# A fused attention and two feed-forward layers on one core: softmax left unscaled, splits and block sums exchanged between two engines

## The chip, the core and the metric

One core of a Trainium2 chip runs the whole program in one launch. The metric is device time in microseconds (us), the median of several runs. TensorE (PE) does matrix products, VectorE (DVE), ScalarE (ACT) and GpSimd (POOL) do elementwise work, and SyncE (SP) issues nearly all DMAs. Each engine runs its own instructions in program order and waits for others by semaphores.

## The reference, cut to what matters

```python
# attention over channels: N = 6016 tokens, C = 256
qn = q / (norm(q, axis=tokens) + 1e-6);  kn = k / (norm(k, axis=tokens) + 1e-6)
s = kn.T @ qn / tau                       # 256 x 256
a = exp(s - s.max(-1));  a /= a.sum(-1) + 1e-9
x = v @ a                                 # tokens x 256
# first feed-forward layer, 2048 wide
h = x @ w_in;  x = maximum(0.01 * h, h) @ w_out
# second feed-forward layer, 1536 wide
out = (1 / (1 + exp(-(x @ w_gate))) * (x @ w_val)) @ w_out2
```

q, k and v are float32; the five weight matrices arrive as float64 and are turned into float32 inside the program.

## The kernel before, in words

**Start.** q and k come in groups of 128-token rows (`GROUPS`, in units of 128 tokens). For each group ACT squares both, DVE adds the squares to two accumulators (GpSimd takes the last ones of k), and TensorE adds to two 128x256 halves of k.T q. `ORDER` says which group's products follow which group's arrival; the second half lags behind, and `REST` holds its last products, which run after the norm products (L334). Then come the norms, the scaled scores (`scaled`, L355), exp with its row sum in `zs`, and `turned` (L371): 1/sum on DVE, the row scaled by it, two transposes on TensorE, a copy to `eT`.

**W'.** x is never formed. Since x @ w_in = v @ (a @ w_in), the kernel makes W' = a @ w_in block by block: for block j of 256 columns, `w_prime` (L212) does four float32 products into a PSUM bank `wp`, one half of the rows per half of `eT`.

**Weights.** A `Unit` is one 256x256 float64 block (512 KB). `act` (L168) takes two ACT instructions, x and c, and `join` (L175) three on DVE: L178, L179 and L183. W_in blocks are joined into `win`, blocks of w_out are joined and split.

**Splits.** Every operand of the large products is a pair: high = a rounded copy (ACT), low = the value minus high (a subtraction on DVE or GpSimd). A product of two pairs is three matmuls: low x high, high x low, high x high.

**Pairs and groups.** Tokens go in 6 pairs of two 512-token halves (the last of 2 x 448). For each layer and pair, a group j takes 256 hidden columns: 8 groups per pair in layer one, 6 in layer two. `Core` does a 256x256 by 256x1024 block product with 7 block products and block sums; the first pair of layer one uses `Plain` (L478) with 8 block products and no sums, because its W' is only then being made. A group's hidden blocks are named 22, 12, 11, 21. Each gets its activation (ACT, `g`), then `parts` (L514): high `gh` on ACT, low `gl` on the engine named. TensorE multiplies them with w_out one group later (`sum`, L531): `sums(("22", "12"))` stands after the first half of the next group's core and `sums(("11", "21"))` after that.

**What sets the order.** The order is written out by hand (`manual_schedule`); there is no planner. In a group of the first pair (from L672) TensorE does core.begin (banks d, b), the previous group's 22 and 12, `w_prime(j + 2)` into bank b, the previous 11 and 21, core.end (banks a, c). DVE's row is: join two units, four block sums of W' (L242 to L245, used by later pairs), the low parts of W' (L236), the low part of those sums (L251). GpSimd makes all four `gl` (L518).

**Late weights.** During pairs two to five the 18 units of layer two are joined on DVE (`late_join`, L581); the 12 gate and value units also get four block sums (`sums_of`, L185, on DVE at L190), then high and low parts, and go to DRAM. Each stands in DVE's row ahead of the group's `c12` (L470), which empties bank c for the next group.

**End.** After the last group its four hidden blocks are split, multiplied in the order 22, 12, 11, 21 and stored.

Of the kernel before, what the change touches and what calls it, by code (L numbers as in the profile page):

```python
# [22 lines left out]
P = 128  # L23
# [15 lines left out]
GROUPS = [1, 1, 2] + [4] * 10 + [2, 1]  # L39

ORDER = [
# [3 lines left out]
]  # L45
REST = [[(1, 10), (1, 13)], [(1, 11), (1, 12), (1, 14)]]

WIDTH = [4] * 10 + [2, 2, 2, 1, 1]
# [10 lines left out]
def attention_two_ffn(ctx, tc, q, k, vT, tau, w_in, w_out1, w_gate, w_val, w_out2, outT):  # L59
# [93 lines left out]
    class Unit:  # L153
# [21 lines left out]
        def join(self, out=None):  # L175

            s = cv.tile([P, CH], I32, tag="s", name="s", bufs=3)
# [4 lines left out]
            out = s if out is None else out  # L182
            nc.vector.tensor_tensor(out, s, self.c, ALU.add)  # L183
# [28 lines left out]
    def w_prime(j, wp, halves=range(KC)):  # L212

        w = f32(win[j]).rearrange("p (a b) -> p a b", a=2)
        for i in halves:
            for jj in range(KC):
                nc.tensor.matmul(  # L217
                    wp[:, i * 256:(i + 1) * 256], eT[i][:, jj * P:(jj + 1) * P], w[:, jj, :],
                    start=jj == 0, stop=jj == KC - 1,
                )  # L220
        return wp
# [15 lines left out]

    def block_sums(src, out):

        a, o = blocks(src), blocks(out)  # L240
        tt = nc.vector.tensor_tensor
# [15 lines left out]
    with tc.manual_schedule():  # L257


        with ExitStack() as actx:  # L260
# [61 lines left out]
            ins[0].load(ew)  # L322
            tok.load()
            ins[1].load(ew)
# [4 lines left out]
            win[0] = ins[0].join()  # L329
# [15 lines left out]
            nc.vector.tensor_scalar_mul(rn[:, 0:2], rn[:, 0:2], rt)  # L345
            products(REST[0])

# [33 lines left out]

            scaled(0)
            ins[1].act()
            win[1] = ins[1].join()
            for w in (B12, B22):
                tok.high(w)
                tok.low(w, nc.gpsimd)
            products(REST[1])
            turned(0)
            for w in (B11, B21):  # L390
                tok.high(w)
                tok.low(w, nc.gpsimd)
            wp0 = [bank("y2", "wp"), bank("y3", "wp")]
            for j in range(2):
                w_prime(j, wp0[j], [0])
            scaled(1)
            outs1[0].act()
            turned(1)
            o1_0 = outs1[0].join()
            for j in range(2):  # L400
                w_prime(j, wp0[j], [1])
                new_weights(j, s_a)
                split_blocks(j, wp0[j])
            ins[2].act()
# [228 lines left out]
        for i, (kind, p, j) in enumerate(groups):  # L633
# [44 lines left out]
            if kind == 1 and p == 0:  # L678
                core = Plain(s1_t[j], a21_t[j], g.tok, n)
                core.begin()  # L680

                for w, jj, u in acted:
# [5 lines left out]
                acted = [soon.pop(0) for _ in range(min(2, len(soon)))]  # L688

                def act(which):  # L690
                    for _, _, u in acted[which:which + 1]:
                        u.act()
                        load_next()

                adds()
                sums(("22", "12"))
                wp = w_prime(j + 2, bank("b", "wp")) if j + 2 < G1 else None
                g22, g12 = g.act(core.c22, tmp_tile("g22")), g.act(core.c12, tmp_tile("g12"))
                g.parts("22", g22, nc.gpsimd)
                g.parts("12", g12, nc.gpsimd)  # L700
                act(0)
                if j == 0:
                    for jj in range(2):
                        wt = tmp_tile("wt")
                        nc.scalar.copy(wt, wp0[jj])
                        unsummed.append((jj, wt))
                now = [(jj, block_sums(wt, tmp_tile("ws"))) for jj, wt in unsummed[:2 if j else 1]]
                unsummed = unsummed[len(now):]
                highs()
                lows()  # L710
                if wp is not None:
                    wt = tmp_tile("wt")
                    nc.scalar.copy(wt, wp)
                    new_weights(j + 2, s_a if j + 2 < 3 else s_b)
                    split_blocks(j + 2, wt)
                    unsummed.append((j + 2, wt))
                for jj, o in now:
                    split_sums(jj, o)
                sums(("11", "21"))
                finish()  # L720
                core.end()
                g.leaky("11", core.c11, tmp_tile("g11"), nc.gpsimd)
                g.leaky("21", core.c21, tmp_tile("g21"), nc.gpsimd)
                act(1)
# [51 lines left out]
            else:  # L776
# [37 lines left out]
                g.parts("11", gated("11", val.a), nc.gpsimd)  # L814
# [33 lines left out]
```

## Time and profile before

| | |
|---|---|
| median of 3 runs | 1112.7 us (1111.83 to 1113.08) |
| the profiled execution | 1111.23 us |
| its span, first to last instruction | 1109.5 us |
| DVE busy | 792.9 us (71%) |
| ACT busy | 602.1 us (54%) |
| POOL busy | 524.7 us (47%) |
| granted TensorE clock | full in every slice |
| bytes moved | 84.00 MB, mean 76 GB/s |

The page divides the span into 40 slices. TensorE's row reads 9 tenths or more in all but the first, the fifth and the last, which have 8. The shares of busy time are means over stages that differ, so the rows below are read stage by stage: the start (0 to 68 us), the first pair (68 to 157 us), the pairs with late weights (157 to 600 us), the rest, and the end.

### The profile page before, as it was taken

The page shows a single profiled execution, that of the slowest core. Times are in us where ns is not written, and L with a number is a line of the kernel's source. Part 1 is how long each engine was busy: PE and PEld are TensorE (multiplying, and loading weights), DVE is VectorE, ACT ScalarE, POOL GpSimd, SP SyncE. Part 2 cuts the span into 40 slices and gives each one's busy share as a digit, 9 for nine tenths or more (in the row PEclk, how much of TensorE's full clock was granted, in tenths as well). Part 3 has the DMA queues.
Part 4 walks back from the last instruction along what each step waited for, and adds up shares of the span by engine and source line. Part 5 has one row for each costly group of instructions (what it writes and reads, how often), then busy time and mean ns, then how long its engine had stood idle before and what let it go on. Part 6 is the DMA issues. An engine that isn't in the chain of part 4 may idle for free.

```text
span 1109.5 us, 13984 instructions
## 1 busy us (share of the span) xinstructions
PE 1083.4 (98%) x4842; PEld 906.1 (82%) x4842; DVE 792.9 (71%) x1100; ACT 602.1 (54%) x1043; POOL 524.7 (47%) x392
## 2 busy tenths in 40 slices
PE   8999899999999999999999999999999999999998
PEld 7778787878877788879988888888887888888997
DVE  7889956776786776783456687677677777668765
ACT  6666656676666676675564444444444344444433
POOL 0346566556655655656534434433433433443333
PEclk9999999999999999999999999999999999999999
DMA  9713212214223223209431002002002001100100
GB/s 349 248 38 114 78 57 76 79 77 149 91 76 109 86 91 124 90 34 360 161 118 40 1 0 77 1 1 76 1 1 77 1 1 38 34 1 1 39 1 34
DMA packets 31207, 84.00 MB, mean 76 GB/s; under 512 B 2976, under 2 KB 5792, under 8 KB 31136
## 3 DMA queue, kind: packets, MB, share of 16 engines
q1 hardware_dynamic: 31104, 83.11, 21.2%
q8 instruction: 38, 0.62, 0.2%
q14 instruction: 33, 0.27, 0.1%
q0 software_dynamic: 32, 0.00, 0.0%
HBM read 56.62 MB, written 26.48 MB: 75 GB/s over the span
## 4 chain that ended last, share of the span: by engine, by line
PE 86%; DVE 8%; issue 3%; ACT 2%; DMA 1%; POOL 1%; SPq 0%; DVEq 0%; ACTq 0%; POOLq 0%
PE c L441 13%; PE d L441 13%; PE a L441 12%; PE y L545 12%; PE y L542 12%; PE y L543 12%; PE b L441 6%; PE s L293 3%; DVE s L179 1%; DVE s L178 1%; DVE tok L144 1%; PE wp L217 1%; PE a L492 1%; DVE w L183 1%; DMA qt<-in_q 1%
## 5 line engine op out<-in xcount | busy, mean ns | idle before, releaser
L542 PE MATMUL y<-gh,wo 128*128 128x512 f32 (+1 forms) x672 | 260.1, 387 | 1.3 <-ACT gh L517 1.3
L543 PE MATMUL y<-gh,wo 128*128 128x512 f32 (+1 forms) x672 | 258.8, 385 | 0.0
L518 POOL TENSOR_TENSOR gl<-v,gh 128x512 fp32r<-128x512 f32 (+1 forms) x76 | 106.1, 1396 | 275.8 <-issue 187.2
L545 PE MATMUL y<-gl,wo 128*128 128x512 f32 (+1 forms) x672 | 205.0, 386 | 0.3 <-POOL gl L518 0.2
L441 PE MATMUL c<-tok,s 128*128 128x512 f32 (+1 forms) x672 | 186.7, 386 | 7.8 <-DVE c L470 7.8
L441 PE MATMUL d<-tok,s 128*128 128x512 f32 (+1 forms) x672 | 186.5, 386 | 0.0
L441 PE MATMUL a<-tok,s 128*128 128x512 f32 (+1 forms) x672 | 185.9, 385 | 0.0
L470 DVE TENSOR_TENSOR c<-u,c 128x512 f32<-128x512 f32 (+1 forms) x112 | 75.5, 675 | 134.6 <-PE c L441 129.4
L441 PEld LDWEIGHTS c<-tok,s 128*128 128x128 f32 x672 | 125.6, 188 | 33.5 <-DVE c L470 10.3
L518 POOL TENSOR_TENSOR gl<-g,gh 128x512 fp32r<-128x512 f32 (+1 forms) x72 | 98.0, 1370 | 104.5 <-PE d L441 70.4
L542 PEld LDWEIGHTS y<-gh,wo 128*128 128x128 f32 x672 | 126.2, 188 | 25.5 <-ACT gh L517 2.0
L545 PEld LDWEIGHTS y<-gl,wo 128*128 128x128 f32 x672 | 125.6, 188 | 25.9 <-POOL gl L518 2.8
L518 POOL TENSOR_TENSOR gl<-c,gh 128x512 fp32r<-128x512 f32 (+1 forms) x76 | 99.0, 1303 | 99.4 <-ACT gh L517 66.1
L441 PEld LDWEIGHTS d<-tok,s 128*128 128x128 f32 x672 | 125.6, 188 | 24.6 <-DVE u L475 1.6
L543 PEld LDWEIGHTS y<-gh,wo 128*128 128x128 f32 x672 | 126.2, 188 | 23.4
L441 PEld LDWEIGHTS a<-tok,s 128*128 128x128 f32 x672 | 126.2, 188 | 23.4
L455 DVE TENSOR_TENSOR u<-u,a 128x512 f32<-128x512 f32 (+1 forms) x112 | 75.1, 671 | 39.4 <-PE a L441 31.2
L518 POOL TENSOR_TENSOR gl<-u,gh 128x512 fp32r<-128x512 f32 (+1 forms) x76 | 98.6, 1297 | 0.0
L441 PE MATMUL b<-tok,s 128*128 128x512 f32 (+1 forms) x336 | 92.9, 385 | 0.0
L452 ACT COPY u<-b 128x512 f32<-128x512 f32 (+1 forms) x112 | 64.8, 578 | 47.5 <-PE b L441 47.5
L517 ACT CAST gh<-v 128x512 fp32r<-128x512 f32 (+1 forms) x76 | 46.5, 612 | 79.4 <-DVE v L803 76.2
L458 DVE TENSOR_TENSOR v<-u,c 128x512 f32<-128x512 f32 (+1 forms) x112 | 75.7, 676 | 14.2 <-PE d L441 0.5
(126 smaller groups left out, 1516.8 us busy)
## 6 DMA issues: line engine op xcount, KB each, us to landing
wr<-in_moe_w_out SPq DMA_DIRECT2D x14, 512.0 KB, 4.0
g_d<-st SPq DMA_DIRECT2D x6, 896.0 KB, 3.6
v_d<-st SPq DMA_DIRECT2D x6, 896.0 KB, 3.6
s<-g_d SPq DMA_DIRECT2D x6, 896.0 KB, 5.6
s<-v_d SPq DMA_DIRECT2D x6, 896.0 KB, 6.1
kt<-in_k SPq DMA_DIRECT2D x10, 512.0 KB, 9.7
qt<-in_q SPq DMA_DIRECT2D x10, 512.0 KB, 10.2
x_d<-o SPq DMA_DIRECT2D x20, 256.0 KB, 3.2
```

What stands on the lines that cost most here:

```text
L144: eng.tensor_tensor(t[:, 1], self.part(which), f32(t[:, 0]), ALU.subtract)
L293: nc.tensor.matmul(s_ps[i][:, :C], kt[:, t, i * P:(i + 1) * P], qt[:, t, :], start=i not in begun, stop=gi == ng - 1 and t == GROUPS[gi] - 1,)
L441: nc.tensor.matmul(o[:, :n], self.st[:, w, kind, :], t[:, x, :n], start=first and i == 0, stop=i == 2, skip_group_check=not first,)
L452: nc.scalar.copy(u[:, :n], self.b[:, :n])
L455: nc.vector.tensor_tensor(u[:, :n], u[:, :n], self.a[:, :n], ALU.add)
L458: nc.vector.tensor_tensor(v[:, :n], u[:, :n], self.c[:, :n], ALU.add)
L470: nc.vector.tensor_tensor(t[:, :n], self.u[:, :n], self.c[:, :n], ALU.add)
L517: nc.scalar.copy(gh[:, :n], src[:, :n])
L518: eng.tensor_tensor(gl[:, :n], src[:, :n], f32(gh[:, :n]), ALU.subtract)
L542: nc.tensor.matmul(acc[c, m][:, :n], wo[:, 1, e, s[m]], gh, start=first, stop=False)
L543: nc.tensor.matmul(acc[c, m][:, :n], wo[:, 0, e, s[m]], gh, start=False, stop=False)
L545: nc.tensor.matmul(acc[c, m][:, :n], wo[:, 0, e, s[m]], gl, start=False, stop=stop)
```

## The change

Five edits go together.

1. `GROUPS` begins 1, 1, 2, 2, 2 instead of 1, 1, 2, 4; `ORDER` no longer lets the second half lag in the first seven groups. `REST` keeps 6 and 9 products.
2. `turned` transposes the unscaled exp. 1/sum is computed beside it (`inverse`) and applied when W' leaves PSUM: as `scale` on ACT and as the scalar of one multiply-and-subtract on DVE (`split_half`, `w_evac`). The two halves of the first two W' blocks get banks of their own. W_in block 1 is loaded ahead of the tokens and its `act` moves ahead of the norms; the first join is cut in two.
3. In the first pair `gl` is made by DVE, and the block sums of W' by GpSimd. Token low parts at the start move from GpSimd to DVE.
4. In the first pair both units of a group are acted on and joined in the middle of that group, no longer at the beginning of the next. In group 0 core.end comes ahead of `w_prime(2)`.
5. The block sums of the late gate and value weights go to GpSimd. In the very last group the order is 22, 11, 12, 21, and the low part of 21 is made by DVE.

DVE at the start, from the reciprocal of the first row sum (`z_78`; `z_79` is the second) on. Before:

```order
L372 TENSOR_SCALAR z_78<-z_78 128x1
L373 RECIPROCAL z_78<-z_78 128x1
L374 TENSOR_SCALAR e<-e,z_78 128x256
L362 SCALAR_TENSOR_TENSOR s_sb<-s_123,rn,rq 128x256
L366 TENSOR_REDUCE nm<-s_sb 128x1
L372 TENSOR_SCALAR z_79<-z_79 128x1
L373 RECIPROCAL z_79<-z_79 128x1
L374 TENSOR_SCALAR e<-e,z_79 128x256
```

And now (`tok` are low parts of tokens, `wp` is W' in PSUM, `a_464` and `s` its split parts):

```order
L404 TENSOR_SCALAR z_78<-z_78 128x1
L405 RECIPROCAL z_78<-z_78 128x1
L386 SCALAR_TENSOR_TENSOR s_sb<-s_123,rn,rq 128x256
L390 TENSOR_REDUCE nm<-s_sb 128x1
L143 TENSOR_TENSOR tok<-raw,tok 128x512 x2
L176 TENSOR_SCALAR s<-wr 128x512
L177 SCALAR_TENSOR_TENSOR s<-x,s 128x512
L183 ISA s<-s,c 128x1024
L254 SCALAR_TENSOR_TENSOR a_464<-wp,z_78,a_464 128x128
L254 SCALAR_TENSOR_TENSOR s<-wp,z_78,s 128x128
L404 TENSOR_SCALAR z_79<-z_79 128x1
L405 RECIPROCAL z_79<-z_79 128x1
```

Both scalings of `e` are gone; token low parts and a join stand between the row maximum and the first low parts of W'.

DVE in a middle group of the first pair. Before (`wo` the rounded w_out block, `ws` the block sums of W', `wt` its copy in SBUF):

```order
L201 CAST wo<-s 128x512
L242 TENSOR_TENSOR ws<-wt 128x128
L243 TENSOR_TENSOR ws<-wt 128x128
L244 TENSOR_TENSOR ws<-ws,wt 128x128
L245 TENSOR_TENSOR ws<-wt,ws 128x128
L236 TENSOR_TENSOR a_839<-wt,a_839 128x128
L236 TENSOR_TENSOR s<-wt,s 128x384
L251 TENSOR_TENSOR s<-ws,s 128x512
L178 TENSOR_SCALAR s<-wr 128x512
L179 SCALAR_TENSOR_TENSOR s<-x,s 128x512
L183 ISA s<-s,c 128x1024
```

And now, with the row of the same W' block (`a_875`):

```order
L176 TENSOR_SCALAR s<-wr 128x512
L177 SCALAR_TENSOR_TENSOR s<-x,s 128x512
L183 ISA s<-s,c 128x1024
L206 CAST wo<-s 128x512
L242 TENSOR_TENSOR a_875<-wt,a_875 128x128
L242 TENSOR_TENSOR s<-wt,s 128x384
L549 TENSOR_TENSOR gl<-g_906,gh 128x512
L549 TENSOR_TENSOR gl<-g_912,gh 128x512
L273 TENSOR_TENSOR s<-ws,s 128x512
L549 TENSOR_TENSOR gl<-g_953,gh 128x512
```

Four `ws` rows have left DVE, four `gl` rows have come, and a unit's join stands ahead of the split of W' in the same group.

GpSimd where the first late gate unit (`w_1692`) is joined. Before:

```order
L126 TENSOR_TENSOR sums<-raw 128x1024
L518 TENSOR_TENSOR gl<-v,gh 128x512
L518 TENSOR_TENSOR gl<-g_1700,gh 128x512
L518 TENSOR_TENSOR gl<-c_1706,gh 128x512
L518 TENSOR_TENSOR gl<-u,gh 128x512
```

And now:

```order
L125 TENSOR_TENSOR sums<-raw 128x1024
L549 TENSOR_TENSOR gl<-v,gh 128x512
L195 TENSOR_TENSOR w_1692<-w_1692 128x128 x4
L549 TENSOR_TENSOR gl<-g_1722,gh 128x512
L549 TENSOR_TENSOR gl<-c_1728,gh 128x512
L549 TENSOR_TENSOR gl<-u,gh 128x512
```

The four sums stand between the low parts of 22 and 11, and wait for the join on DVE.

```diff
-GROUPS = [1, 1, 2] + [4] * 10 + [2, 1]
+GROUPS = [1, 1, 2, 2, 2] + [4] * 9 + [2, 1]
...
-WIDTH = [4] * 10 + [2, 2, 2, 1, 1]
+WIDTH = [4] * 11 + [2, 2, 2, 1, 1]
...
     def sums_of(w8):
...
-            nc.vector.tensor_tensor(w8[:, o], w8[:, a], w8[:, b], op)
+            nc.gpsimd.tensor_tensor(w8[:, o], w8[:, a], w8[:, b], op)
...
+    def split_half(j, i, wp):
+
+        src = wp.rearrange("p (a b) -> p a b", a=2)
+        st, a = s1_t[j], a21_t[j]
+        todo = [(st[:, :, 1:3], src)]
+        if i == 0:
+            todo = [(a[:, :, 0:1], src[:, 0:1]), (st[:, :, 0:1], src[:, 1:2])]
+        for o, x in todo:
+            nc.scalar.activation(o[:, 0], x, AF.Copy, scale=zs[i])
+        for o, x in todo:
+            nc.vector.scalar_tensor_tensor(o[:, 1], x, zs[i], f32(o[:, 0]), ALU.mult, ALU.subtract)
+
+    def w_evac(wt, wp):
+        for i in range(KC):
+            nc.scalar.activation(wt[:, i * 256:(i + 1) * 256], wp[i], AF.Copy, scale=zs[i])
+
     def block_sums(src, out):
...
-        tt = nc.vector.tensor_tensor
+        tt = nc.gpsimd.tensor_tensor
...
             ins[0].load(ew)
+            ins[1].load(ew)
             tok.load()
-            ins[1].load(ew)
...
             ins[0].act()
-            win[0] = ins[0].join()
+            ins[1].act()
+            ins[0].begin_join()
...
             def turned(i):
-                nc.vector.tensor_scalar_add(zs[i], zs[i], EPS_SUM)
-                nc.vector.reciprocal(zs[i], zs[i])
-                nc.vector.tensor_scalar_mul(e_sb[i], e_sb[i], zs[i])
...
             products(REST[1])
             turned(0)
...
+            wp0 = [[bank(f"y{2 + j}", "wp")[:, :256]] for j in range(2)]
+            for j in range(2):
+                w_half(j, 0, wp0[j][0])
+                new_weights(j, s_a)
+            scaled(1)
+            ins[2].act()
+            turned(1)
+            for w in (B12, B22):
+                tok.low(w, nc.vector)
+            o1_0 = outs1[0].join()
+            split_half(0, 0, wp0[0][0])
+            inverse(1)
+            for j in range(2):
+                wp0[j].append(w_half(j, 1, bank(f"y{j}", "wp")[:, :256]))
+            split_half(0, 1, wp0[0][1])
...
                 sums(("22", "12"))
+                if j == 0:
+                    core.end()
+                wp = w_prime(j + 2, bank("b", "wp")) if j + 2 < G1 else None
+                g22, g12 = g.act(core.c22, tmp_tile("g22")), g.act(core.c12, tmp_tile("g12"))
+                g.parts("22", g22, nc.vector)
+                g.parts("12", g12, nc.vector)
+
+                units = [soon.pop(0) for _ in range(min(2, len(soon)))]
+                for _, _, u in units:
+                    u.act()
+                    load_next()
...
+                if (p, j) == (NP_ - 1, count - 1):
+                    g.parts("12", gated("12", val.c12()), nc.gpsimd)
+                    g.parts("21", gated("21", val.c21()), nc.vector)
+                    g.sum(("22", "11", "12", "21"))
+                    g.store()
+                    break
```

## Rows read from the trace of the kernel before

**Rows 1.** The page, busy time of TensorE (us, share of the span, instructions).

```profile
PE 1083.4 (98%) x4842; PEld 906.1 (82%) x4842; DVE 792.9 (71%) x1100; ACT 602.1 (54%) x1043; POOL 524.7 (47%) x392
```

**Rows 2.** Waits of TensorE, whole run: us in total, times, longest.

```profile
PE c L441 <- DVE c L470: 7.8, 6, 1.8
PE wp L217 <- DVE s L183: 4.7, 3, 2.4
PE s L293 <- DMA qt<-in_q: 3.2, 2, 2.5
PE eT_ps L377 <- DVE e L374: 2.5, 2, 1.4
```

**Rows 3.** Timeline, 11 to 43 us: start, duration, engine, instruction [idle before, releaser].

```profile
11.87 30.89 PE L293 MATMUL s<-qt,kt 128*128 128x256 f32 x142 [2.54 <-DMA qt<-in_q]
...
42.28 0.42 DVE L314 TENSOR_TENSOR accq<-accq,s 128x256 f32<-128x256 f32 x1 [0.50 <-ACT x L171]
...
42.96 0.25 PE L334 MATMUL nrm<-ones,accq 128*128 128x1 f32 x1
```

**Rows 4.** Timeline, 40 to 70 us: softmax, W' and the first group.

```profile
46.51 4.05 PE L293 MATMUL s<-qt,kt 128*128 128x256 f32 x18
...
47.69 0.51 ACT L368 ACTIVATE e<-s_sb,nm 128x256 f32<-128x256 f32 x1
...
50.70 0.97 DVE L374 TENSOR_SCALAR e<-e,z 128x256 f32<-128x256 f32 x1
...
51.73 0.44 PE L377 MATMUL eT_ps<-ident,e 128*128 128x128 f32 x2 [1.17 <-DVE e L374]
...
52.63 1.99 PE L217 MATMUL wp<-s,eT 128*128 128x256 f32 x8 [0.46 <-ACT eT L380]
...
54.53 1.30 DVE L374 TENSOR_SCALAR e<-e,z 128x256 f32<-128x256 f32 x1
...
55.98 0.41 PE L377 MATMUL eT_ps<-ident,e 128*128 128x128 f32 x2 [1.35 <-DVE e L374]
...
58.66 0.97 PE L492 MATMUL d<-tok,a 128*128 128x512 f32 x3
...
63.11 1.97 PE L217 MATMUL wp<-s,eT 128*128 128x256 f32 x8 [1.02 <-DVE s L183]
```

**Rows 5.** Chain that ended last, 60 to 80 us: start, us, what.

```profile
67.82 1.36 PE d L492 x6
...
73.27 1.80 PE wp L217 x8
```

**Rows 6.** Groups by form, first pair (65 to 157 us): count, busy us, mean ns.

```profile
L243 DVE TENSOR_TENSOR ws<-wt 128x128 f32<-128x128 f32 x8 | 10.1, 1258 | 0.0
...
L251 DVE TENSOR_TENSOR s<-ws,s 128x512 fp32r<-128x512 f32 x8 | 5.4, 683 | 0.0
...
L242 DVE TENSOR_TENSOR ws<-wt 128x128 f32<-128x128 f32 x8 | 2.7, 338 | 2.1 <-ACT wt L705 2.1
```

**Rows 7.** The same, GpSimd.

```profile
L518 POOL TENSOR_TENSOR gl<-g,gh 128x512 fp32r<-128x512 f32 x30 | 44.2, 1494 | 14.9 <-ACT gh L517 8.5 <-issue 3.4 <-PE d L492 2.8
```

**Rows 8.** Windows: us, busy us (instructions) of PE, PEld, DVE, ACT, POOL, clock, DMA.

```profile
100.00:120.00 20.00, 18.77 (x83) 15.34 (x82) 19.42 (x22) 11.23 (x22) 13.95 (x10) 1.00 0.25 81
200.00:400.00 200.00, 194.38 (x852) 158.95 (x851) 149.62 (x196) 129.90 (x221) 115.52 (x82) 1.00 0.27 91
```

**Rows 9.** Timeline, 317 to 329 us, a late w_out unit.

```profile
326.69 0.96 PE L441 MATMUL c<-tok,s 128*128 128x512 f32 x3 [1.49 <-DVE c L470]
```

**Rows 10.** The same, 361 to 373 us, a gate or value unit.

```profile
368.29 1.99 DVE L190 TENSOR_TENSOR w<-w 128x128 f32<-128x128 f32 x4
...
370.93 0.97 PE L441 MATMUL c<-tok,s 128*128 128x512 f32 x3 [1.78 <-DVE c L470]
```

**Rows 11.** Groups by form, GpSimd, whole run: its smallest two-input form.

```profile
L314 POOL TENSOR_TENSOR acck<-acck,s 128x256 f32<-128x256 f32 x3 | 2.6, 877 | 0.2
```

**Rows 12.** Timeline, the end.

```profile
1101.27 0.47 PE L542 MATMUL y<-gh,wo 128*128 128x448 f32 x1 [1.30 <-ACT gh L517]
```

More of the change, by code (lines that the diff above doesn't have):

```diff
@@ L181, in join, with end_join @@
             )
-            out = s if out is None else out
-            nc.vector.tensor_tensor(out, s, self.c, ALU.add)
-            return out
+        def end_join(self, out=None):
+            out = self.s if out is None else out
+            nc.vector.tensor_tensor(out, self.s, self.c, ALU.add)
+            return out
+        def join(self, out=None):
+            self.begin_join()
+            return self.end_join(out)
     def sums_of(w8):
@@ L210, in attention_two_ffn, with w_half, w_prime @@
     win = {}
-    def w_prime(j, wp, halves=range(KC)):
+    def w_half(j, i, o):
         w = f32(win[j]).rearrange("p (a b) -> p a b", a=2)
[L215 to L221, printed above, removed]
+        for jj in range(KC):
+            nc.tensor.matmul(
+                o, eT[i][:, jj * P:(jj + 1) * P], w[:, jj, :], start=jj == 0, stop=jj == KC - 1
+            )
+        return o
+    def w_prime(j, wp):
+        return [w_half(j, i, wp[:, i * 256:(i + 1) * 256]) for i in range(KC)]
     ins = [Unit(cols(w_in, j)) for j in range(G1)]
@@ L380, in turned, with inverse @@
                 nc.scalar.copy(eT[i], eT_ps[:, :C])
+            def inverse(i):
+                nc.vector.tensor_scalar_add(zs[i], zs[i], EPS_SUM)
+                nc.vector.reciprocal(zs[i], zs[i])
             scaled(0)
-            ins[1].act()
             win[1] = ins[1].join()
+            inverse(0)
+            outs1[0].act()
             for w in (B12, B22):
                 tok.high(w)
-                tok.low(w, nc.gpsimd)
             products(REST[1])
             turned(0)
+            wp0 = [[bank(f"y{2 + j}", "wp")[:, :256]] for j in range(2)]
[13 more added lines that the diff above has]
+            split_half(0, 1, wp0[0][1])
             for w in (B11, B21):
                 tok.high(w)
[L392 to L404, printed above, removed]
+            split_half(1, 0, wp0[1][0])
+            split_half(1, 1, wp0[1][1])
+            for w in (B11, B21):
+                tok.low(w, nc.vector)
             win[2] = ins[2].join()
@@ L680, in attention_two_ffn @@
                 core.begin()
-                for w, jj, u in acted:
+                adds()
+                sums(("22", "12"))
+                if j == 0:
[8 more added lines that the diff above has]
+                    load_next()
+                if j == 0:
+                    for jj in range(2):
+                        wt = tmp_tile("wt")
+                        w_evac(wt, wp0[jj])
+                        unsummed.append((jj, wt))
+                now = [(jj, block_sums(wt, tmp_tile("ws"))) for jj, wt in unsummed[:2 if j else 1]]
+                unsummed = unsummed[len(now):]
+                for w, jj, u in units:
                     if w == "in":
@@ L687, in attention_two_ffn @@
                         split_rows(u.join(), o1_t[jj], nc.gpsimd)
[L688 to L708, printed above, removed]
                 highs()
@@ L716, in attention_two_ffn @@
                     unsummed.append((j + 2, wt))
+                sums(("11", "21"))
+                finish()
+                if j:
+                    core.end()
+                g.leaky("11", core.c11, tmp_tile("g11"), nc.vector)
+                g.leaky("21", core.c21, tmp_tile("g21"), nc.vector)
                 for jj, o in now:
                     split_sums(jj, o)
[L719 to L724, printed above, removed]
             elif kind == 1:
```

16 lines of the change are left out of this document (8 added, 8 removed), and 3 rows, old and new, of the table ORDER.

## The prediction

> **What bounds the kernel now.** I read the page first: TensorE is busy 98% of the span, 1083.4 of 1109.5 us [rows 1]. So nothing that merely frees another engine pays; at most the 26 us in which TensorE stands idle can be won. The list of TensorE's waits says where four of these lie: 7.8 us in six waits for DVE's c12 (L470), 4.7 in three for a join (L183), 3.2 for q, 2.5 for the scaled softmax [rows 2]. Then the timelines show which stage each falls in, and the windows whether the engine waited for is full there. In the first pair DVE is busy 19.42 of 20 us while TensorE is not [rows 8]: there DVE sets the pace. From 200 to 400 us DVE has 50 us to spare [rows 8], and the waits are places where too much stands ahead of one instruction.
>
> **First loads.** TensorE idles 2.54 us for q at 11.87 [rows 3], and smaller loads let its products start sooner. But the products end at 11.87 + 30.89 = 42.76, and DVE's last add of squares ends at 42.28 + 0.42 = 42.70; the norm product of q needs it and starts at 42.96 [rows 3]. TensorE runs in order, so products that finish sooner wait there. DVE's tail of adds is the same as before (the last three groups of four, then two and one). I cost this edit at 0; DVE's adds hide it. If the last add also comes sooner, at most the 2.54 are won; if the four extra small loads cost transfer rate, a little is lost. Range -0.3 to +2.5.
>
> **Softmax unscaled, start up to group 1.** Before, the last product ends at 46.51 + 4.05 = 50.56, and group 1's first matmul starts at 67.82 [rows 4, 5]: 17.26 us. The work of TensorE in between is 24 block matmuls, four times 1.36 per six = 5.44; three W' products at 1.80 (73.27 shows one without a stall) = 5.40; two pairs of transposes, 0.44 + 0.41 [rows 4, 5]. Together 11.69, so 5.57 is lost. Now the first exp, begun at 47.69, is ready before 50.56, and the scaling (0.97, begun at 50.70, and 1.30 at 54.53 [rows 4]) stands on no path to a transpose. So the waits of 1.17 and 1.35 in front of the transposes go, and DVE reaches the second half's scores 1 us sooner. What stays: both copies of the transposes to SBUF on ACT, 0.46 each [rows 4]. What is late next: the low parts. On DVE the low parts of two token blocks (0.68 each, as L251 [rows 6]) and a join of three instructions now stand ahead of the first low part of W', and `inverse(1)` behind it holds ACT's scaled copy of the second half; behind that copy ACT has two token highs, block 1's copies and the group's activations, for which TensorE waits next. I let TensorE lose 0.55 there. So 0.92 + 0.55 = 1.47 stays of 5.57: 4.1 won. core.end ahead of `w_prime(2)` covers the join that made TensorE wait 1.02 at 63.11 [rows 4]; that is part of the 5.57. Bounds: all but the copies, 4.65; or only the two waits on the scaling, 1.17 + 1.35 = 2.5, less 1 for the new queue on ACT and DVE, 1.5. Loading W_in block 1 ahead of the tokens puts three token transfers one block later on SP's queue; they are first read at the token highs, after block 1's x and c, so I give it nothing.
>
> **First pair.** Of the 4.7 waited for joins, 4.7 - 1.02 = 3.7 lie here [rows 2, 4]. Per group DVE loses four block sums (mean 0.338 to 1.258 each [rows 6]: 1.4 to 5.0) and gains four low parts at 0.683, as L251 of the same shape [rows 6], 2.7. GpSimd loses four at 1.494 [rows 7], 6.0, and gains four block sums. Their price on GpSimd isn't in the trace: the nearest form, two inputs of 256 columns, took 0.877 [rows 11]; below lies DVE's 0.338, above GpSimd's 1.494 for 512 columns. I take 0.6, 2.4 a group. The same block sum takes 0.338 or 1.258 on DVE as L242 or L243 [rows 6], which differ in what GpSimd does beside them. The Trainium skill (SBUF — State Buffer, Who interferes with whom) says that a DVE instruction with two SBUF inputs and a GpSimd one that reads SBUF exclude each other for the whole instruction; the two means agree. By that rule alone the sum over both engines counts, and it falls from 6.0 + 1.4 to 2.7 + 2.4, so relief would come all the same.
>
> The joins also stand half a group earlier than the product that needs them. So the 3.7 go. A new wait comes in group 1: ACT has six half-size scaled copies and four unit copies in group 0, its activations of group 1 stand behind them, and the W' product into bank b waits for the second. I let this cost 0.6, between nothing and one W' product, 1.8. The low parts on DVE are needed by TensorE half a group later and more. Net 3.1, between 1.5 and 3.7.
>
> **Late weights.** Two of the six waits, 2.9 together, are at w_out units, like the 1.49 at 326.69 [rows 9]; no block sum stands there and nothing changes. The other four, 7.8 - 2.9 = 4.9, are at gate and value units. At 368.29 four sums take 1.99 directly ahead of c12, and TensorE then waits 1.78 [rows 10]: without them c12 comes in time. On GpSimd they stand between the low parts of 22 and of 11, and make 11, 12 and 21 later by four sums and the wait for the join; 12 is wanted early in the next group. GpSimd idles 84 us in 200 [rows 8], so I allow 0.5 for this: 4.4 won, between 2 and 6.
>
> **End.** TensorE waits 1.30 for the high part of 12 [rows 12]. With 11 ahead of it, six matmuls fill that, and 12's gate no longer stands behind c21. 21's low part moves to DVE beside 12's on GpSimd. I take 1.1, between 0.4 and 1.8.
>
> **Sum.** 0 + 4.1 + 3.1 + 4.4 + 1.1 = 12.7. Against the profiled execution, 1111.23 (span 1109.5 and 1.7 around it), that makes 1098.5; this execution was 1.5 under the median, so from 1112.7 it makes 1100.0, which I predict. With the inner bounds it lies between 1097 and 1102.5.
>
> **Rivals.**
> *The work only changes places.* DVE and GpSimd exclude each other, and DVE, now with the low parts that TensorE waits for, stays full in the first pair: 3.1 becomes 0, and GpSimd's block sums cut the late gain in half, 2.2. 4.1 + 2.2 + 1.1 = 7.4: 1105.3. For it: DVE at 19.42 of 20 [rows 8] and the 1.258 [rows 6]. Against: a low part is less than half as long on DVE as on GpSimd (0.683 against 1.494). The Trainium skill (Perfetto Trace Analysis, Optimizing Scalar/DVE Operations) warns that moving operations between these two might not help, because they share a port; this is that case, and the exchange here goes the other way for the larger operations.
> *The start is eaten by its new queue.* The order on ACT and DVE behind the second exp is long; the start gives 1.5 and not 4.1: 1102.6. For it: each engine is in order and every new instruction ahead of a split counts. Against: the rows show DVE and ACT with gaps there only because of the scaling.
> *More goes than I count.* The last add of squares comes sooner (another 1.7), and the waits at w_out units go because their neighbours ran on time (2.9): 1095.4.
> *Slower: GpSimd becomes the bound.* If a sum of 128 columns costs GpSimd as much as 512 columns (a fixed cost), 1.494, the four take 6.0 in each of the 12 gate and value groups. A group of 45 matmuls takes 10.2 us, so GpSimd's idle time [rows 8] is 84.5 x 10.2 / 200 = 4.3 a group. 1.7 too much twelve times is 20, with nothing won in the first pair or the late ones: 1112.7 - 5.2 + 20 = 1127. It decides from 4.3 / 4 = 1.1 us a sum. Against it: 256 columns took 0.877 [rows 11].
>
> **Chances.** The forecast 0.60, work changes places 0.13, start eaten 0.14, more than counted 0.08, slower 0.05. The range, 1095.5 to 1106, takes in all but the slower rival and the far ends. No change (within 0.2%, 2.2 us, about what a measurement of this kernel can tell) would need several of the terms to fail together: 0.03. Faster 0.92, slower 0.05.
>
> **What would show it.** Right: no wait of a transpose for DVE; group 1's first matmul of bank d at 63.7 or so; no wait of a W' product for a join; c12 waits left at two w_out units alone; in the end TensorE's wait for gh under 0.4. The norm products still start close to 42.9, and TensorE waits there. A block sum on GpSimd lasts under 0.9. Wrong: norm products a microsecond earlier (first loads pay); W' products waiting for ACT's activation into bank b in several groups; `y` matmuls waiting for `gl` from DVE or GpSimd; DVE still at 95% in the first pair with TensorE waiting.

## The result and the profile after

The changed kernel takes 1094.26 us (median of 6 runs, 1093.51 to 1095.26) against 1112.99 for the kernel before (1111.83 to 1115.58): a ratio of 0.9829, 95% interval 0.9816 to 0.9841. The gain is 18.7 us where 12.7 were forecast; 1094.26 lies 1.2 us below the low end of the range.

The page after, busy time, answers to [rows 1]:

```profile
span 1091.4 us, 13956 instructions
...
PE 1081.2 (99%) x4842; PEld 907.2 (83%) x4842; DVE 774.6 (71%) x1059; ACT 604.6 (55%) x1055; POOL 522.2 (48%) x435
```

TensorE's waits after, whole run, answer to [rows 2] (us in total, times, longest):

```profile
PE c L472 <- DVE c L501: 2.9, 2, 1.5
PE idle L298 <- DVE ones L293: 1.1, 1, 1.1
PE wp L221 <- ACT eT L401: 0.9, 2, 0.5
PE s L315 <- DMA qt<-in_q: 0.9, 2, 0.7
PE nrm L357 <- DVE accq L336: 0.2, 1, 0.2
```

Gone are the 4.7 for joins and the 2.5 for the scaled rows; 7.8 for c12 became 2.9. The listed waits that went add up to 13.4 (4.9 + 4.7 + 2.5, and 1.3 at the end), about the forecast; q's 3.2 became 0.9 besides. The two spans differ by 18.1. So the waits were named rightly and something beside their listed length was won.

The start after, timeline (start, duration, engine, instruction), answers to [rows 3 to 5]:

```profile
40.34 0.50 PE L357 MATMUL nrm<-ones,acck 128*128 128x1 f32 x4
41.00 0.61 PE L357 MATMUL nrm<-ones,accq 128*128 128x1 f32 x4 [0.16 <-DVE accq L336]
...
44.57 4.05 PE L315 MATMUL s<-qt,kt 128*128 128x256 f32 x18
48.46 0.38 PE L398 MATMUL eT_ps<-ident,e 128*128 128x128 f32 x2
49.30 1.99 PE L221 MATMUL wp<-s,eT 128*128 128x256 f32 x8 [0.46 <-ACT eT L401]
51.13 0.38 PE L398 MATMUL eT_ps<-ident,e 128*128 128x128 f32 x2
...
61.35 1.04 PE L523 MATMUL d<-tok,a 128*128 128x512 f32 x3
```

The transposes follow the products at once, and group 1's first d comes soon after its W' product. Stage by stage, profile against profile and by the chain as in the prediction, the 18.1 us are:

| stage | forecast | between the two profiles |
|---|---|---|
| up to q's norm product (42.96, now 41.00) | 0 | 1.96 |
| last product to group 1's first d (17.26, now 13.08) | 4.1 | 4.18 |
| first pair from there (89.61, now 85.50) | 3.1 | 4.11 |
| pairs two on, to the third of the last three d products (940.96, now 934.50) | 4.4 | 6.46 |
| end (11.11, now 9.70) | 1.1 | 1.41 |

The windows after, in the columns of [rows 8]:

```profile
100.00:120.00 20.00, 20.00 (x90) 16.72 (x89) 19.31 (x25) 16.85 (x34) 12.42 (x12) 1.00 0.30 87
200.00:400.00 200.00, 198.40 (x873) 163.07 (x872) 144.10 (x172) 135.03 (x230) 131.85 (x113) 1.00 0.28 98
```

In the first pair DVE is as full as before, 19.31 of 20 us, and TensorE no longer waits for it. The GpSimd block sum of a late unit, whose price the prediction had to bound from [rows 11], and the low part of g on DVE in the first pair:

```profile
L195 POOL TENSOR_TENSOR w<-w 128x128 f32<-128x128 f32 x48 | 21.2, 463 | 17.3 <-DVE w L183 16.4
```

```profile
L549 DVE TENSOR_TENSOR gl<-g,gh 128x512 fp32r<-128x512 f32 x29 | 28.2, 1008 | 3.3 <-ACT gh L548 3.3
```

### The profile page after: what moved, and what is told of

It reads as the page before. It is cut to its first block, busy times and chain, and to the rows that moved or that the text cites. A ratio compares the mean times of both kernels' runs of the same rounds, so it can differ in the third digit from the quotient of the medians.

```text
span 1091.4 us, 13956 instructions
## 1 busy us (share of the span) xinstructions
PE 1081.2 (99%) x4842; PEld 907.2 (83%) x4842; DVE 774.6 (71%) x1059; ACT 604.6 (55%) x1055; POOL 522.2 (48%) x435
## 4 chain that ended last, share of the span: by engine, by line
PE 92%; DVE 4%; DMA 2%; ACT 1%; issue 1%; SPq 0%; ACTq 0%; DVEq 0%
PE c L472 13%; PE y L576 13%; PE d L472 13%; PE y L573 13%; PE y L574 13%; PE a L472 13%; PE b L472 7%; DMA kt<-in_k 2%; PE wp L221 1%; PE a L523 1%; PE c L523 1%; PE b L523 1%; PE d L523 1%; DVE accq L336 1%; PE s L315 1%
## 5 line engine op out<-in xcount | busy, mean ns | idle before, releaser
L491 DVE TENSOR_TENSOR v<-v,d 128x512 f32<-128x512 f32 (+1 forms) x112 | 75.7, 676 | 11.7
```

Source lines behind the costliest of these rows:

```text
L491: nc.vector.tensor_tensor(v[:, :n], v[:, :n], self.d[:, :n], ALU.add)
```

## The experiments

Times are medians; the changed kernel, timed again beside three of them, took 1093.47, and its ten timed runs have a median of 1093.9. The experiments ran on four chips. Runs of the kernel before whose clock stayed up have a median of 1110.0 on one of them and 1111.2 on another, so differences under about 1 us between runs that are not said to be beside each other say little, and I go by the traces there. "Excess" is worked out from the starts of neighbouring matmuls in the traces: what they stand further apart than the 0.227 of unhindered 512-column matmuls, summed around one wait. "Matmul for matmul" compares the starts of the same matmuls in two traces.

### First loads

The changed kernel with GROUPS, ORDER, REST and WIDTH of before, and the kernel before with those of the changed one:

```
-GROUPS = [1, 1, 2, 2, 2] + [4] * 9 + [2, 1]
+GROUPS = [1, 1, 2] + [4] * 10 + [2, 1]
```

> The changed kernel with the group sizes and the product order of the kernel before, all else as changed. Theory A (DVE's adds of squares run without a gap from the first groups of four on, one per 1.28 us as the loads do; whoever starts them 1.4 us sooner ends them that much sooner): the norm product of q goes back from 41.00 to about 42.9 and the run takes 1.9 to 2.0 us longer than the changed kernel, about 1096.2. Theory B (the prediction's step: the end of the adds doesn't depend on the first loads): no change, 1094.3, norm product of q still near 41.0.

> The kernel before with only the new group sizes and product order. Theory A: its norm product of q starts near 41.0 instead of 42.96 and it takes 1.9 us less than before, about 1111.0. Theory B (the adds hide it): same time as before, 1112.9.

Measured: 1093.96, no loss that a median shows, and 1111.14 beside 1111.79, ratio 0.9994 (0.9982 to 1.0005). The 1.9 of theory A falls. With the old loads the first square of four units came at 9.21, against 10.54 in the first profile of before, though the loads are the same:

```profile
9.21 1.06 ACT L333 ACTIVATE s<-kt 128x1024 f32<-128x1024 f32 x1 [1.05 <-DMA kt<-in_k]
```

```profile
10.54 1.06 ACT L310 ACTIVATE s<-kt 128x1024 f32<-128x1024 f32 x1 [3.03 <-DMA kt<-in_k]
```

The first row is of the changed kernel with old loads, the second of the kernel before. The norm product of q, with old loads in the changed kernel, then with new loads in the kernel before:

```profile
41.60 0.59 PE L358 MATMUL nrm<-ones,accq 128*128 128x1 f32 x4
```

```profile
40.75 0.61 PE L333 MATMUL nrm<-ones,accq 128*128 128x1 f32 x4 [0.17 <-DVE accq L313]
```

So much of the 1.96 was chance, but not all. The three profiles with old loads have this product at 41.60, 42.12 and 42.96, the fifteen with new loads between 40.58 and 41.58, 41.0 in the mean. By these means the edit is worth 1.2, by the two medians taken beside each other 0.6, and the interval of that ratio takes in nothing as well as 1.2. I take 0.6, somewhere from 0 to 1.2: theory B's "no change" isn't shown either.

### The kernel before once more

> The kernel before, unchanged, for a second profile and the granted clock of each of its runs. Theory A (two things of the first profile were chance: its first load of four units came late, at 10.54, and its clock didn't fall; most runs lose over 1 us more to a clock that falls to half behind one of TensorE's long waits): the first square of four units starts near 9.2, the norm product of q near 41.6, and runs with a mean clock of 0.998 or less take 1.5 to 3.5 us longer than those at 1.000. Theory B (the first profile is typical): 10.5, 42.9, and no relation between clock and time.

Measured: 1112.48 (1110.79 to 1114.09, 12 runs); the profiled one has a mean clock of 0.995. Its first square of four units starts at 9.24, as theory A has it, but its q norm product at 42.12, half a us later than A says: when the first load lands is not the whole of it. The clock's part of theory A holds. The profile shows what the first profile did not. TensorE behind the wait at 371.89 of the timeline, and the windows of 1 us around it (busy us of PE, PEld, DVE, ACT, POOL; granted clock; DMA):

```profile
371.89 0.96 PE L441 MATMUL c<-tok,s 128*128 128x512 f32 x3 [1.78 <-DVE c L470]
372.69 1.23 PE L441 MATMUL d<-tok,s 128*128 128x512 f32 x3
373.73 0.63 PE L542 MATMUL y<-gh,wo 128*128 128x512 f32 x1
...
376.66 0.39 PE L543 MATMUL y<-gh,wo 128*128 128x512 f32 x1
```

```profile
371.00:372.00 1.00, 0.11 (x1) 0.11 (x1) 0.90 (x3) 0.13 (x1) 0.00 (x0) 1.00 0.50 208
372.00:373.00 1.00, 1.00 (x4) 0.67 (x5) 1.00 (x2) 0.91 (x2) 0.00 (x0) 1.00 0.02 7
373.00:374.00 1.00, 1.00 (x4) 0.79 (x3) 0.87 (x2) 0.97 (x3) 0.71 (x1) 0.59 0.00 0
374.00:375.00 1.00, 1.00 (x3) 0.72 (x3) 0.73 (x2) 1.00 (x2) 1.00 (x2) 0.50 0.00 0
375.00:376.00 1.00, 1.00 (x4) 0.80 (x3) 0.73 (x1) 1.00 (x3) 0.82 (x1) 0.50 0.00 0
376.00:377.00 1.00, 1.00 (x5) 0.82 (x4) 1.00 (x2) 0.97 (x3) 0.00 (x0) 0.70 0.00 0
377.00:378.00 1.00, 1.00 (x6) 0.83 (x5) 0.37 (x1) 1.00 (x2) 0.98 (x1) 1.00 0.49 201
```

For 1.78 up to 371.89 TensorE waits; from 373.2 to 376.6 its granted clock stands at the lower level (0.50, 1.2 GHz), and a `y` matmul lasts 0.63 where one at the full clock lasts 0.39. The excess around this wait is 3.75; in the first profile, the clock at 1.00, it was 2.15. This execution has two more falls, at the waits that end at 50.89 (52.3 to 55.7) and at 127.64 (127.4 to 130.8). Of 66 runs of the kernel before in this study, 20 have a mean clock of 0.999 or 1.000, median 1110.7; 46 are lower, median 1113.2; the same order holds on each of the two chips that have many runs of both kinds (1110.0 against 1112.8, 1111.2 against 1113.3). Of ten runs of the changed kernel none is below 0.999.

### Late block sums back on DVE

```
-            nc.gpsimd.tensor_tensor(w8[:, o], w8[:, a], w8[:, b], op)
+            nc.vector.tensor_tensor(w8[:, o], w8[:, a], w8[:, b], op)
```

> The changed kernel with the four block sums of a late gate or value unit back on DVE. Theory A (each listed wait for c12 costs TensorE about 0.35 more than its listed length, and each of four such waits comes back): 6.0 to 6.5 us longer than the changed kernel, 1100.3 to 1100.8. Theory B (the listed lengths are the cost): 4.9 us longer, 1099.2. The listed waits of c for c12 should read about 7.8 in six by both.

Measured: 1102.39, 8.5 more than the changed kernel's median, above both; its two runs with a mean clock of 0.999 and 1.000 took 1101.43 and 1102.10. Its waits of c for c12:

```profile
PE c L472 <- DVE c L501: 8.6, 7, 1.8
```

The five that are new have an excess of 1.18, 1.90, 1.16, 1.19 and 3.77; the last is the one listed at 1.78, with a fall of the clock behind it (0.50 from 364 to 366). A small wait of 0.57 that the changed kernel has in the same place goes: 8.6 in all, 7.0 without the fall (1.6 by the same wait in the first profile of before).

### What a wait costs: six waits made on purpose

c12 of the value product written five times, then four times, in six groups:

```
-                c12, c21 = val.c12(), val.c21()
+                c12, c21 = val.c12(5 if p in (2, 3, 4) and j in (1, 3) else 1), val.c21()
```

> The changed kernel with c12 of the value product written five times instead of once in six groups of the second network (pairs three to five, groups two and four), so that TensorE waits for it there; the repeats change nothing in the result. By the durations 4 x 0.69 of DVE less about 1.2 of slack make six waits of 1.5 each, 9 listed. Theory A: each costs its listed length and about 0.35 for the refill, 11 in all, in runs whose clock stays at 1.000; and a fall of the clock to half, some 3.5 us long and worth 1.7, follows some of them. Theory B: listed lengths alone, 9, and no fall of the clock, since a wait of 1.5 is no different from one of 0.5.

> As the six stalls, with c12 written four times instead of five, so that each of the six waits is 0.7 shorter, about 1.0 listed. Theory A (refill costs about 0.38 a wait whatever its length; the clock's fall follows only the longer waits): 6 x (1.0 + 0.38) = 8.3 us longer than the changed kernel, mean clock 0.999 or 1.000. Theory B (a fall follows each wait with some chance, whatever its length): runs at 0.998 or less, 10 us longer and more. Theory C (listed length only): 6.0 longer.

Measured: 1109.63 with five (mean clock 0.996 to 0.998 in every run) and 1101.77 with four (0.999 or 1.000). The first wait of each trace, and the one of the longer six that a fall follows:

```profile
764.25 0.97 PE L472 MATMUL c<-tok,s 128*128 128x512 f32 x3 [1.62 <-DVE c L502]
796.62 0.96 PE L472 MATMUL c<-tok,s 128*128 128x512 f32 x3 [2.05 <-DVE c L502]
```

```profile
763.76 0.98 PE L472 MATMUL c<-tok,s 128*128 128x512 f32 x3 [0.91 <-DVE c L502]
```

The short waits, 0.91 and 0.98 in turn, have an excess of 1.28 and 1.35 each: 0.37 above what is listed. Six times 1.32 are 7.9; measured 8.3 against the changed kernel beside it. The long ones have 1.99 to 2.08 in five places, the 1.62 of the first being 1.99 in excess: again 0.37 more. The sixth, listed at 2.05, has 4.02: the fall adds 1.6. Theory A holds in both, though the longer waits came out at 1.62 to 2.05 and not at 1.5, so that the six without a fall make 12.6 and not its 11. Where the 0.37 lies can be read from the starts. 0.16 is how the view counts: it lets the matmul ahead of the wait last its full 0.39 before the idle time begins, while unhindered starts stand 0.227 apart. The rest lies behind the wait: the second matmul starts 0.34 after the first and the fifth 0.31 to 0.33 after the fourth, so 0.11 and about 0.09 more than 0.227. What holds these two up is open. The word refill in the theories covers both parts.

### The exchange and the joins of the first pair

Low parts of g (22, and likewise 12, 11 and 21) on GpSimd and block sums on DVE again; then, in another run, the joins back in the next group, where the second unit's x and c on ACT go behind the group as well:

```
-                g.parts("22", g22, nc.vector)
+                g.parts("22", g22, nc.gpsimd)
...
-        tt = nc.gpsimd.tensor_tensor
+        tt = nc.vector.tensor_tensor
```

> The changed kernel with the first pair's low parts of g back on GpSimd and the block sums back on DVE; the joins stay half a group ahead. Theory A (the exchange relieves DVE, which set the pace of the first pair): waits of W' products for joins come back, 2 to 4 us longer than the changed kernel, and pairs two on are unchanged. Theory B (the joins' place alone carries the gain of the first pair): under 0.5 us longer, and the first pair still lasts 85.5 from group 1's first d to pair two's first b.

> The changed kernel with the first pair's joins back where the kernel before has them (in the next group, ahead of its W' product); the exchange of low parts and block sums stays. Theory A (both halves of the edit are needed): W' products wait for joins again, 2 to 4 us listed, and the run takes 2 to 6 us longer than the changed kernel, 1096 to 1100. Theory B (the exchange gives DVE so much room that the joins' place doesn't matter): under 0.5 us longer, no wait of a W' product for a join.

Measured: 1104.14 and 1098.41. Waits in the first, then in the second:

```profile
PE y L576 <- POOL gl L549: 6.5, 4, 3.4
```

```profile
PE wp L221 <- ACT gh L548: 3.1, 4, 1.6
...
PE wp L221 <- DVE s L183: 0.9, 1, 0.9
```

Theory A of each names the direction, with other waits than I named: in the first, `y` matmuls wait for GpSimd; in the second, 3.1 of the 4.0 are waits for ACT's `gh`, and only 0.9 for a join. The first b of pair two, in the same order:

```profile
155.96 0.84 PE L472 MATMUL b<-tok,s 128*128 128x512 f32 x3
```

```profile
151.67 0.84 PE L472 MATMUL b<-tok,s 128*128 128x512 f32 x3
```

From group 1's first d (61.35 and 61.43 in these timelines) the first pair lasts 94.6 and 90.2, against 85.7 in the changed kernel and 89.6 in the kernel before: 8.9 longer without the exchange, 4.6 longer without the earlier joins, and 3.9 longer with neither (4.1 by the chain of the table). So the earlier joins alone would have made it slower by 5.0, the exchange alone by 0.6; the kernel before has another start, so these two are read across kernels. The gain belongs to the two together. Which half of the exchange, the low parts or the block sums, carries it was not tried.

### Softmax scaled, and the old order at the start

Rows scaled ahead of the transposes again, with W' copied out with a factor of 1 and all else as changed; then also x and c of the second W_in unit behind the exp and the token low parts on GpSimd; then that order with unscaled rows. Of the first edit:

```
             def turned(i):
+                nc.vector.tensor_scalar_add(zs[i], zs[i], EPS_SUM)
+                nc.vector.reciprocal(zs[i], zs[i])
+                nc.vector.tensor_scalar_mul(e_sb[i], e_sb[i], zs[i])
...
```

> The changed kernel with the softmax rows scaled by 1/z on DVE ahead of the transposes again, and W' copied out with a factor of 1. All other moves at the start stay. Theory A (the scaling in front of the transposes is what the start's 4.2 us came from): the two waits in front of the transposes come back at about 1.2 and 1.35, 2.3 to 2.6 us longer than the changed kernel. Theory B (the order of joins, token splits and a/c products carries the start, and the scaling would hide beside the products that are still running): under 1 us longer.

> The changed kernel with the rows scaled ahead of the transposes and with the old order at the start: x and c of the second W_in unit behind the exp, token low parts on GpSimd right behind their high parts. Theory A (the scaling cost time only because DVE came late to it, behind a join that waited for x, and ran 0.97 and 1.30 instead of 0.35 beside GpSimd's low parts; the order took that away, so leaving the scaling out won nothing on top): waits of 1 to 1.4 in front of both transposes come back, 2 to 3 us longer than the changed kernel. Theory B (the start's gain lies in neither, but in the a and c products ahead of the third W' product and the half-wise copies): under 0.7 us longer.

> The changed kernel, rows unscaled, with the old order at the start alone (x and c of the second W_in unit behind the exp, token low parts on GpSimd). Theory A (either edit, the order or the unscaled rows, is enough to free the transposes): no wait of a transpose for DVE and under 0.7 us longer than the changed kernel. Theory B (GpSimd's low parts slow DVE's adds and splits at the start in any case): 1 to 2.5 us longer, with waits of d, b or a products for low parts.

Measured: 1094.26, 1095.63 and 1095.82. In the first, theory B holds: the scaling costs nothing. Its scaling and transposes, then those with the old order, then the waits with the old order and unscaled rows:

```profile
47.46 0.35 DVE L398 TENSOR_SCALAR e<-e,z 128x256 f32<-128x256 f32 x1
...
48.12 0.38 PE L401 MATMUL eT_ps<-ident,e 128*128 128x128 f32 x2
```

```profile
48.87 0.35 DVE L397 TENSOR_SCALAR e<-e,z 128x256 f32<-128x256 f32 x1
...
49.28 0.44 PE L400 MATMUL eT_ps<-ident,e 128*128 128x128 f32 x2 [0.56 <-DVE e L397]
...
52.09 1.11 DVE L397 TENSOR_SCALAR e<-e,z 128x256 f32<-128x256 f32 x1
...
53.35 0.41 PE L400 MATMUL eT_ps<-ident,e 128*128 128x128 f32 x2 [1.17 <-DVE e L397]
```

```profile
50.02 1.99 PE L221 MATMUL wp<-s,eT 128*128 128x256 f32 x8 [1.15 <-ACT eT L400]
...
56.09 0.96 PE L521 MATMUL d<-tok,s 128*128 128x512 f32 x3 [0.46 <-DVE s L254]
```

With the new order DVE reaches the scaling at 47.46, while products run until 48.28. In the old order DVE stood behind a join that waited for x, and later ran beside GpSimd's low parts, 1.11 instead of 0.35 ([rows 4] have 0.97 and 1.30). From the last product's end to group 1's first d (in the timelines, 12.73 in the changed kernel): 12.79 scaled, 14.76 scaled in the old order, 13.87 unscaled in the old order. So leaving the scaling out wins 0.9 in the old order and nothing in the new one; the order wins 2.0 with scaled rows and 1.1 with unscaled ones. The last kernel fits neither theory whole: no transpose waits for DVE, as A has it, but it is 1.1 longer, as B has it, since both copies of the transposes stand behind token high parts on ACT and a d product waits 0.5 for a low part.

### The third W' product ahead of the a and c products

```
-                if j == 0:
-                    core.end()
                 wp = w_prime(j + 2, bank("b", "wp")) if j + 2 < G1 else None
```

> The changed kernel with the a and c products of the first group behind the third W' product again, as the other groups have them. Theory A (in the kernel before, 2.2 of the start's 4.2 us came from the third W' product and the groups' first products waiting behind the queue on DVE and ACT, and the a and c products now cover it): a wait of the third W' product for a join or for an activation into bank b comes back, 1 to 2.5 us longer. Theory B (the earlier joins alone make it come in time): under 0.4 us longer.

Measured: 1097.75 against 1093.47 beside it. TensorE:

```profile
59.74 3.40 PE L221 MATMUL wp<-s,eT 128*128 128x256 f32 x8 [2.81 <-DVE s L183]
62.57 1.72 PE L523 MATMUL a<-tok,s 128*128 128x512 f32 x4
```

The wait comes back, longer than the 1.02 of before: this join now stands on DVE behind two token low parts as well. A fall of the clock follows (3.40 for a product that takes 1.89), and every run has a mean clock of 0.997 or 0.998. Theory A's mechanism holds. Matmul for matmul the start loses 3.7, of which some 1.6 are the fall; without it the 2.1 lie within theory A's 1 to 2.5. Another 1.2 of this trace arises in the last pair and not here (see the two waits that were left). Of the start's 4.2, order and scaling bring 2.0; I put the other 2.2 down to this edit, though the half-wise copies and the two banks for them were never undone by themselves, and could hold some of it.

### The end

Order and engines of the last group as before (the `break` branch of the diff taken out).

> The changed kernel with the last group's end as before: order 22, 12, 11, 21, all four low parts on GpSimd. Theory A (the end's own term, 1.1 forecast, 1.4 read from the two profiles): 1.1 to 1.5 us longer than the changed kernel, with TensorE's wait for the high part of 12 back at 1.3. Theory B (the end is set by the last copies and stores, and the order of the sums is hidden): under 0.4 us longer.

Measured: 1096.14, 2.2 over the changed kernel's median, and 1.9 over the 1094.26 of the kernel with scaled rows, whose runs stood beside it. The wait is back:

```profile
PE y L573 <- ACT gh L548: 1.3, 1, 1.3
```

Matmul for matmul, against the trace of the changed kernel, 1.9 is lost across this wait and the next one, for GpSimd's low part of 12, and 0.3 is won back behind them: 1.6 in all. Theory A's mechanism, a little larger.

### The two waits that were left

The join of a w_out unit moved behind c12 and c21 on DVE:

```
                 for w, jj, u in joined:
-                    late_join(w, u)
+                    if w != "o":
+                        late_join(w, u)
...
                 c12, c21 = core.c12(), core.c21()
+                for w, jj, u in joined:
+                    if w == "o":
+                        late_join(w, u)
```

> The changed kernel with the join of a late w_out unit moved behind c12 and c21 on DVE; it left two waits of c for c12, 1.5 each. Theory A (a wait costs TensorE what is listed and about 0.35 more, and now and then a clock fall behind it): both waits go and the run takes 3.5 to 4 us less than the changed kernel, about 1090.5, with every mean clock at 1.000. Theory B (the listed lengths are the whole cost): 2.9 us less, 1091.4. Theory C (the join, now ahead of the next group's adds, makes those late instead): waits of the same sum return at the next group's products, within 1 us of 1094.3.

> The changed kernel, unchanged, beside the next one. Theory A (its two waits of 1.5 are followed by a fall of the clock seldom or never, unlike the waits of 1.8 to 2.4 of the kernel before): median 1094 to 1094.6, mean clock 0.999 or 1.000 in every run, spread under 2.5 us. Theory B (falls of the clock are as frequent as before): some runs at 0.998 or less and 1.5 to 2 us longer.

> The late join of w_out units once more, beside the changed kernel on one chip. Theory A (excess of matmul starts around the two waits, 1.86 and 1.52): 3.0 to 3.5 us less than the changed kernel beside it. Theory B (listed lengths 2.9 are the upper limit, and the 2.5 between the two profiled spans is the true gain): 2.3 to 2.7 less.

Measured: 1091.15; then, beside each other, 1090.46 and 1093.47 for the changed kernel, whose clock was 0.999 or 1.000 in every run, as theory A of the second text has it (its median is 0.5 under the one named there). Listed waits for c12 fall from 2.9 to 0.2:

```profile
PE c L472 <- DVE c L501: 0.2, 1, 0.2
```

3.0 less: the low end of the last text's theory A, and near the 2.9 of the first text's theory B; C falls. The listed lengths are not told apart from more by this median alone. This version beats both kernels: 0.9788 of the kernel before (0.9772 to 0.9805). Across the two waits its trace wins 3.3, matmul for matmul, 0.4 more than is listed; but in the last pair of the second network, from 1019 us to the end, its matmuls stand 2% further apart than the changed kernel's (0.207 instead of 0.203 for 448 columns), at a granted clock of 1.00, which takes 1.2 back. Both profiles of this version and that of the third W' product ahead have such a stretch, the other fifteen have not. Why is open, and so is why the medians still differ by 3.0 where these traces, their starts aside, leave 2.1.

## Why the prediction was wrong, point by point

The direction and most places were right: every wait that the text said would go went, and the two at w_out units stayed. What failed is the price: the text counted a wait of TensorE at its listed length, less an allowance, and carried the distance between profile and median over unchanged. In runs whose clock did not fall the medians are 1110.7 and 1093.9, 16.8 apart where 12.7 were forecast; the falls make up the rest of the 18.7, 1.9.

- **First loads (0).** Too low, by about 0.6 (0 to 1.2). The profile's 1.96 is in good part a late landing in the first profile. Of the text's reason, products that finish sooner do wait at the norm product, but only 0.16: when DVE's adds end follows from when the loads land, which I took as fixed. The text's sign of being wrong, norm products a microsecond earlier, came.
- **Start (4.1; 4.18).** The sum was right by luck, its cause wrong. The step "the scaling stands on no path to a transpose, so the waits of 1.17 and 1.35 go" names the edit that wins nothing on top of the new order and 0.9 without it. The order alone takes these waits away; the rest goes with the a and c products ahead of the third W' product, as far as is shown.
- **First pair (3.1; 4.1).** The two waits for joins, 3.6 and not 3.7, were priced as listed, and a new ACT wait at 0.6; the trace after lists no wait of TensorE there. Each of the two cost about 0.25 more than listed, and ACT's 0.23 of before went as well. The GpSimd block sums took 0.78 to 0.87 beside DVE's low parts, not 0.6, and those 1.008 in the mean instead of 0.683; neither is waited for. The text gave exchange and joins a gain each; the runs give it only to both.
- **Late weights (4.4; 6.5).** The step that failed first: "the other four, 7.8 - 2.9 = 4.9", with 0.5 off for GpSimd. Four waits cost their 4.9 and about 0.37 each that is not listed, 6.4, and GpSimd at 0.463 a sum cost nothing. The six made-up waits show the same price.
- **End (1.1; 1.4, or 1.6 by undoing it).** The listed 1.30 was priced at 1.1; it cost 1.57 in matmul starts.
- **From the profile to the median.** The second failure: "this execution was 1.5 under the median, so from 1112.7 it makes 1100.0" carried over an offset that was largely the falls of the clock behind the kernel's longer waits. The profile from which I read happened to have none, and in ten runs of the changed kernel there were none: its profiled execution lies 0.75 under its median. The two profiled executions are 17.7 apart, the medians 18.7.

Of the rivals, "more goes than I count" had the time (1095.4) but only part of the cause: the last add does come sooner, by less than its 1.7, and the w_out waits stayed. The rival of work that only changes places has its price refuted, since the first pair won 4.1 with DVE as full as before; half of its idea holds, for DVE's low parts do run longer beside GpSimd, and the exchange alone would have won nothing.

## What to carry to other kernels

Price a wait of TensorE at more than is listed (here 0.25 to 0.45 more), and look over the mean clock of all runs, not only of the profiled one, before an offset between profile and median is carried over. A remedy can be worth nothing beside another for the same wait, and two edits that are harmless or harmful alone can pay together: undo them one at a time. A stage that ends earlier in one profile proves no gain until another profile of the same kernel shows the same start.

## What the runs showed of the hardware

- At some waits of TensorE the granted clock falls to 1.2 GHz for about 3.4 us, about 1.6 us lost each time: at waits listed at 1.78, 2.05, 2.43 and 2.81, and once behind one of 1.18 with one of 0.46 right after it. It is not certain: the 1.78 of [rows 10], the 2.4 of [rows 2] and the 3.4 for GpSimd's low part had none in their executions. None was seen at the single waits of 0.9 to 1.70 of these traces. That the waits bring the falls is shown by the six made-up ones: falls in all seven runs with the longer, in none of five with the shorter.
- With one and the same load sequence the first 512 KB tile was there for ACT at 9.2 us in two executions and at 10.5 in a third.
- DVE's 128x256 scaling took 0.35 alone and 0.97 to 1.30 beside GpSimd's subtractions. Its 128x512 subtraction took 0.68 to 0.69 where GpSimd stood still, 0.94 to 0.95 beside GpSimd's block sums, and 1.78 to 2.89 beside its operations on 512 and 1024 columns of tokens in the same pair; the 1.008 is a mean of all these. Where low parts on DVE and block sums on GpSimd ran in turn (68.9 to 73.2 us in the changed kernel), one of each took 0.87, against 0.60 and 0.42 from start to start for either alone.
